# Decode attention over a cached K and V: the first load cut in two, a small load on another queue, the last loads in other pieces

## The chip, the cores and the metric

The kernel runs on one core of one Trainium2 chip. The metric is the device time of one execution in microseconds (us). The kernel before was run three times: 1307.24, 1308.48 and 1308.63 us, median 1308.48 us.

## The reference

One decode step for 2 sequences: attention with 32 heads of size 128 over a cache of 8192 positions, times a gate that an MLP computes, added to the input. All arrays are float32.

```python
def _A_ref(x, k_cache, v_cache, wq, wo):            # x: 2 x 1 x 512
    q = (x @ wq).reshape(B, Sq, 32, 128)             # heads first after a transpose
    scores = einsum("bhqd,bhkd->bhqk", q, k_cache) * (128 ** -0.5)
    p = softmax(scores, axis=-1)
    o = einsum("bhqk,bhkd->bhqd", p, v_cache)
    return o.reshape(B, Sq, 4096) @ wo
def _B_ref(x, w1, b1, w2, b2):                       # w1: 512 x 1376, w2: 1376 x 512
    h = gelu(layernorm(x) @ w1 + b1)
    return h @ w2 + b2
xn = layernorm(x)
out = x + _A_ref(xn, k_cache, v_cache, wq, wo) * silu(_B_ref(xn, w1, b1, w2, b2))
```

K and V hold 268 MB each, the weights another 22 MB. Each K and V element is used once, so a step is mostly the reading of them.

## The kernel before

**Tiles.** The 64 pairs of sequence and head are taken two at a time: 32 steps, each with one K tile and one V tile of 128 partitions x 128 positions x 128 floats (8.39 MB). Each half of the partitions holds one head, each partition 64 KB that lie in one piece in memory. A load moves one row per partition, and the 16 DMA engines share the 128 rows, 8 each.

**Buffers.** `kpool` has two buffers; wq, the 32 K tiles, one late V tile and wo take turns in them. `vpool` has one buffer. At the start it is `boot`, which holds w1, w2, x, b2 and scratch; then the V tiles follow in it. So k1 can be loaded when the projection of the queries (L241) has read wq, v0 when nothing uses `boot` any more, k2 when VectorE (DVE) is done with k0, v1 when TensorE (PE) is done with v0.

**A step** (L354 to L399). DVE multiplies K by the query in two halves (L279), sums over the head size (L284) and takes the maximum (L288). PE and ScalarE (ACT) turn that into exponentials (L305, L307, L312). PE multiplies them with V, 32 matmuls over 4 positions each (L327); `columns`, `spread` and `place` add the result into OA. The order of all instructions is written out by hand: each engine takes its own in the order of the program.

**Queues.** All large loads are issued by SyncE (SP) on its queue, in the order of the program: w1 (L98), the first 1280 rows of w2 (L99), the last 96 rows of w2 (L100), wq (L101), k0 in two halves, then k1, v0, k2, v1 and so on through `load` (L60). ACT issues five small ones on its own queue: x (L96), b1 and its tail (L107, L108), b2 (L109), and one row of the output at the end. A load waits on its issuing engine for whatever must be done before: the buffer's last reader, or a landing whose semaphore it uses again (there are eight of these for all loads).

**The start.** DVE and ACT compute two layer norms of x (L152 to L158; the square root L156 on ACT needs its function table loaded, as the copy L175 does before it). PE transposes the result, multiplies it with w1 (L196), DVE adds b1 and its tail (L202) and computes the gelu with a tanh from ACT (L207), PE multiplies with w2 (L215) and adds b2 (L218), ACT and DVE finish the gate. Then PE projects the queries from wq (L241), gathers them (L251) and spreads the first (L262); DVE's first multiply (L279) waits for that.

**The end.** The V tile of the last step is loaded in five pieces of 32, 32, 32, 16 and 16 positions (`PIECES`, L71), wo in five pieces of 8, 8, 8, 6 and 2 of its 32 rows per partition (`WO_PIECES`, L72; a row is 2 KB per partition, 262 KB in all). Each piece has its own semaphore, so the matmuls on it (L327, L419) start when it has landed. The final product (L419) takes 4 matmuls for each of the 32 rows of wo, 8 instructions in the trace; DVE multiplies by the gate and adds x (L423, L424), and SP and ACT write the two rows of the output (L427).

Of the kernel before, what the change touches and what calls it, by code (L numbers as in the profile page):

```python
# [8 lines left out]
F32 = mybir.dt.float32  # L9
AF = mybir.ActivationFunctionType  # L10
# [3 lines left out]
EPS = 1e-5  # L14
# [5 lines left out]
def decode_kernel(ctx: ExitStack, tc: tile.TileContext, x, kc, vc, wq, wo, w1, b1, w2, b2, out):  # L20
    nc = tc.nc
    P = 128
    B, H, S, DH = kc.shape
# [15 lines left out]
    NF = F // P  # L39
    FT = F - NF * P  # L40
# [4 lines left out]
    consts = ctx.enter_context(tc.tile_pool(name="consts", bufs=1))  # L45
    kpool = ctx.enter_context(tc.tile_pool(name="kpool", bufs=2))
    vpool = ctx.enter_context(tc.tile_pool(name="vpool", bufs=1))
    small = ctx.enter_context(tc.tile_pool(name="small", bufs=2))
# [9 lines left out]
    def load(dst, src, cuts):  # L58
        for a, e in zip(cuts, cuts[1:]):
            nc.sync.dma_start(dst[:, a:e], src[:, a:e])  # L60
# [5 lines left out]
    def load_v(n, cuts=(0, KP), pool=vpool, tag="v"):  # L66
        V[n] = pool.tile([P, KP, DH], F32, tag=tag, name=f"v{n}")
        load(V[n], vf[n], cuts)


    PIECES = (0, 32, 64, 96, 112, 128)  # L71
    WO_PIECES = (0, 8, 16, 24, 30, 32)  # L72


    wq_sb = kpool.tile([P, ND, H * DH], F32, tag="k", name="wq_sb")
# [3 lines left out]
    def take(p, n):  # L79
        a = used[0]  # L80
        used[0] += n
        assert used[0] <= KP * DH
        return boot[:p, a:a + n]

    w1_sb = take(P, ND * F).rearrange("p (c f) -> p c f", f=F)
    w2_sb = take(P, (NF + 1) * D).rearrange("p (c n) -> p c n", n=D)
    x_sb = take(B, D)
# [5 lines left out]
    z = take(P, P)  # L93
    th = take(P, P)

    nc.scalar.dma_start(x_sb, x.rearrange("b s d -> (b s) d"))  # L96

    nc.sync.dma_start(w1_sb, w1.rearrange("(p c) f -> p c f", p=P))  # L98
    nc.sync.dma_start(w2_sb[:, :NF, :], w2[:NF * P, :].rearrange("(p c) n -> p c n", p=P))  # L99
    nc.sync.dma_start(w2_sb[:FT, NF, :], w2[NF * P:, :])  # L100
    nc.sync.dma_start(wq_sb, wq.rearrange("(p c) n -> p c n", p=P))  # L101
    load_k(0, (0, KP // 2, KP))


    b1_sb = consts.tile([P, NF + 1], F32, name="b1_sb")
    nc.vector.memset(b1_sb, 0.0)
    nc.scalar.dma_start(b1_sb[:, :NF], b1[:NF * P].rearrange("(p c) -> p c", p=P))  # L107
    nc.scalar.dma_start(b1_sb[:FT, NF:NF + 1], b1[NF * P:, None])  # L108
    nc.scalar.dma_start(b2_sb, b2[None, :])  # L109
# [5 lines left out]
    nc.vector.memset(ones, 1.0)  # L115
    srow = consts.tile([1, HP], F32, name="srow")
    nc.vector.memset(srow, SCALE)
    eps_t = consts.tile([B, 1], F32, name="eps_t")
    nc.vector.memset(eps_t, EPS)

    mod = consts.tile([P, R], F32, name="mod")

# [231 lines left out]
    for n in range(N):  # L354
# [11 lines left out]
        if 1 <= n < LATE - 1 or n >= LATE:  # L366
# [7 lines left out]
            elif n == N - 1:  # L374
                load_v(N - 1, PIECES)
        if n >= LATE:
# [24 lines left out]
    wo_sb = kpool.tile([P, OC, D], F32, tag="k", name="wo_sb")  # L401
    load(wo_sb, wo.rearrange("(p c) n -> p c n", p=P), WO_PIECES)

# [51 lines left out]
```

## Time and profile before

| | before |
|---|---|
| median of 3 runs | 1308.48 us (1307.24 to 1308.63) |
| profiled execution, its own time | 1307.31 us |
| span in that execution, first to last instruction | 1305.5 us |
| DVE busy | 1128.8 us (86%) |
| PE busy | 444.4 us (34%) |
| ACT busy | 84.0 us (6%) |
| moved by DMA | 559.76 MB, mean 429 GB/s |
| PE's granted clock, mean | 0.629 of full speed |

The profile page is made from one execution. Its parts give the busy time of each engine, the span in 40 equal slices (each digit the busy tenths of a slice, then the DMA rate in GB/s), the DMA queues (q1 is SP's, q10 ACT's, q8 and q14 carry instructions), the chain of waits that ended last, the costliest groups of instructions, and the DMA issues with their size and the time from issue to landing. A row in order of time reads: start, duration, engine, line, operation, destination <- source, shape, count, and in brackets how long the engine was idle before and what ended that. SPq and ACTq rows are issues of DMAs, not transfers. A row of a stretch of time (such as 1.50:5.00) lists the busy time of PE, PE's weight loads, DVE, ACT and POOL, then PE's granted clock, the DMA engines' mean busy share and the rate in GB/s.

### The profile page before, as it was taken

Reading aid. Unit: us, or ns where it says so; the run is one execution under the profiler, and the core shown is the slowest. Engines: PE = TensorE matmul, PEld = TensorE weight load, DVE = VectorE, ACT = ScalarE, POOL = GpSimd, SP = SyncE. Lnnn points to the kernel's source line nnn. Section 1 sums busy time; section 2 is a strip of 40 time slices with the busy share of each in tenths; the row PEclk is TensorE's granted clock in tenths of the full one; section 3 lists DMA queues with packets and bytes.
Section 4 is the critical chain, followed back from the end, with each engine's and each line's share of the span. In section 5 each row is a group of like instructions: output and inputs, shape, how many; then the busy total and the mean of one; then the engine's idle time right before and its main releaser. Section 6 shows DMA issues by size and latency. Waiting matters only on the chain.

```text
span 1305.5 us, 7374 instructions
## 1 busy us (share of the span) xinstructions
PE 444.4 (34%) x3258; PEld 173.2 (13%) x3258; DVE 1128.8 (86%) x261; ACT 84.0 (6%) x276; POOL 2.8 (0%) x12
## 2 busy tenths in 40 slices
PE   6403333322333322333322333331333332231266
PEld 6101111111111101111100101110111101110013
DVE  1499989888889988889988888988888988889980
ACT  1100000000000000000000000000000000000000
POOL 0000000000000000000000000000000000000000
PEclk9756666556666656666655666655666655665668
DMA  9999999999999999999999999999999999999998
GB/s 398 440 424 442 424 442 422 442 424 442 424 442 424 438 430 436 432 434 432 432 436 428 440 426 438 428 440 424 440 426 440 424 444 422 446 404 426 438 416 339
DMA packets 11509, 559.76 MB, mean 429 GB/s; under 512 B 1515, under 2 KB 1523, under 8 KB 1750
## 3 DMA queue, kind: packets, MB, share of 16 engines
q1 hardware_dynamic: 11208, 559.29, 99.3%
q8 instruction: 25, 0.41, 0.1%
q10 hardware_dynamic: 270, 0.01, 0.0%
q14 instruction: 6, 0.05, 0.0%
HBM read 559.30 MB, written 0.00 MB: 428 GB/s over the span
## 4 chain that ended last, share of the span: by engine, by line
DMA 50%; DVE 48%; PE 1%; ACT 0%; issue 0%; SPq 0%; DVEq 0%
DMA k<-in_A_k_cache_dram 45%; DVE k L279 24%; DVE sc L284 24%; DMA wq_sb<-in_A_wq_dram 3%; DMA wo_sb<-in_A_wo_dram 2%; PE pq L241 1%; DVE nm L297 0%; ACT boot L244 0%; PE acc L419 0%; PE pqa L251 0%; SPq L60 0%; PE pb L262 0%; DVE mx L288 0%; SPq L100 0%; SPq L99 0%
## 5 line engine op out<-in xcount | busy, mean ns | idle before, releaser
L279 DVE TENSOR_TENSOR k<-k,q 128x8192 f32<-128x8192 f32 x64 | 555.5, 8681 | 109.7 <-DMA k<-in_A_k_cache_dram 98.0
L284 DVE TENSOR_REDUCE sc<-k 128x64 f32<-128x8192 f32 x64 | 552.4, 8666 | 0.0
L327 PE MATMUL po<-v,pz 128*8 128x512 f32 x2048 | 295.6, 742 | 202.3 <-DMA v<-in_A_v_cache_dram 202.3
L305 PE MATMUL pn<-nm,srow 1*64 1x1 f32 x128 | 11.7, 246 | 336.4 <-DVE nm L297 336.4
L327 PEld LDWEIGHTS po<-v,pz 128*8 128x8 f32 x2048 | 57.2, 104 | 422.8 <-DMA v<-in_A_v_cache_dram 213.7
L292 PE MATMUL pm<-ident,mx 128*1 128x128 f32 x32 | 11.8, 369 | 222.0 <-DVE Z L342 164.2
L305 PEld LDWEIGHTS pn<-nm,srow 1*64 1x64 f32 x128 | 9.0, 193 | 340.6 <-DVE nm L297 340.5
L334 ACT COPY o<-po 128x512 f32<-128x512 f32 x32 | 18.8, 586 | 516.3 <-PE po L327 516.3
L307 ACT COPY bias<-pn 128x1 f32<-128x1 f32 x32 | 5.1, 160 | 583.2 <-PE pn L305 583.2
L337 PE MATMUL pt<-mod,o 128*128 128x2 f32 x256 | 33.7, 254 | 22.9 <-ACT o L334 22.9
L337 PEld LDWEIGHTS pt<-mod,o 128*128 128x128 f32 x256 | 31.0, 191 | 52.6 <-ACT o L334 52.6
L318 PE MATMUL OA<-ones,ZR 128*128 128x1 f32 x64 | 18.6, 359 | 51.8 <-ACT ZR L315 51.8
L292 PEld LDWEIGHTS pm<-ident,mx 128*1 128x1 f32 x32 | 2.5, 79 | 224.4 <-issue 189.2
L312 ACT ACTIVATE pz<-sc,bias 64x128 f32<-64x128 f32 x64 | 25.5, 399 | 1.4
L318 PEld LDWEIGHTS OA<-ones,ZR 128*128 128x128 f32 x64 | 15.8, 307 | 54.5 <-ACT ZR L315 54.5
L262 PE MATMUL pb<-q_all,ident 64*64 64x128 f32 x128 | 21.6, 438 | 0.3 <-ACT q_all L253 0.3
L342 DVE TENSOR_TENSOR Z<-blk,pt 128x8 f32<-128x8 f32 x32 | 4.9, 152 | 18.4 <-PE pt L337 18.4
L196 PE MATMUL ph<-yT,boot 128*128 128x2 f32 (+1 forms) x88 | 19.5, 359 | 0.8 <-DMA boot<-in_B_w_dram 0.8
L196 PEld LDWEIGHTS ph<-yT,boot 128*128 128x128 f32 (+1 forms) x88 | 19.4, 317 | 0.9 <-ACT yT L166 0.9
L202 DVE TENSOR_TENSOR gh<-ph,b_sb 128x22 f32<-128x22 f32 x1 | 0.2, 181 | 21.0 <-PE ph L196 21.0
L350 PE MATMUL OA<-mod,Z 128*128 128x32 f32 x64 | 15.3, 332 | 4.4 <-DVE Z L342 4.3
L350 PEld LDWEIGHTS OA<-mod,Z 128*128 128x128 f32 x64 | 15.7, 304 | 4.8 <-DVE Z L342 4.8
(81 smaller groups left out, 119.5 us busy)
## 6 DMA issues: line engine op xcount, KB each, us to landing
k<-in_A_k_cache_dram SPq DMA_DIRECT2D x2, 4096.0 KB, 46.9
v<-in_A_v_cache_dram SPq DMA_DIRECT2D x3, 2048.0 KB, 19.2
wo_sb<-in_A_wo_dram SPq DMA_DIRECT2D x3, 2048.0 KB, 22.1
boot<-in_B_w_dram SPq DMA_DIRECT2D x1, 2752.0 KB, 9.7
boot<-in_B_w_dram SPq DMA_DIRECT2D x1, 2560.0 KB, 15.9
v<-in_A_v_cache_dram SPq DMA_DIRECT2D x2, 1024.0 KB
wo_sb<-in_A_wo_dram SPq DMA_DIRECT2D x1, 1536.0 KB
wo_sb<-in_A_wo_dram SPq DMA_DIRECT2D x1, 512.0 KB, 29.5
```

The costliest lines, as they stand in the source:

```text
L196: nc.tensor.matmul(ph[:w.shape[1], f * B:(f + 1) * B], w, yT[:, c, :], start=(c == 0), stop=(c == ND - 1))
L262: nc.tensor.matmul(p[HP * s:HP * (s + 1), :], w, q_all, start=True, stop=True)
L279: nc.vector.tensor_tensor(out=k, in0=k, in1=qb, op=ALU.mult)
L284: nc.vector.tensor_reduce(out=SC[n][:, a:e], in_=K[n][:, a:e, :], axis=AX.X, op=ALU.add)
L292: nc.tensor.transpose(p[:1, :], MX[n], ident)
L305: nc.tensor.matmul(p[HP * s:HP * (s + 1), :1], srow, nm[:, s:s + 1], start=True, stop=True)
L312: nc.scalar.activation(PZ[n % 3][r, :, s, :], sc[r], AF.Exp, bias=bias[r], scale=SCALE, accum_out=rs[r])
L318: nc.tensor.matmul(OA[:, b, OC:], ZR[:, a:a + P], ones[:, :1], start=False, stop=False)
L327: nc.tensor.matmul(po[R * j:R * j + U * JW, :], pz[:, t].rearrange("p s j -> p (s j)"), v[:, t * JW:(t + 1) * JW, :].rearrange("p j d -> p ...
L334: nc.scalar.copy(o4, PO[n % 2])
L337: nc.tensor.matmul(PT[n][:, :U], o4[:, i * DH:(i + 1) * DH], mod[:, i:U * JW:JW], start=(i == 0), stop=(i == JW - 1))
L350: nc.tensor.matmul(OA[:, b, :OC], Z[:, a:a + P], mod, start=False, stop=(n == N - 1))
```

## The change

Five edits, none to what is computed:

- w1 is loaded in two pieces: partitions 0 to 15 (one row for each of the 16 DMA engines), then 16 to 127.
- The last 96 rows of w2 go from SP's queue to ACT's, right behind x.
- `eps_t` is set first on DVE, and ACT computes a square root of it into a scratch tile ahead of everything else. With it the table for the square root is loaded ahead of x, whose load ACT issues next; the separate table load of the first copy (L175) is no longer in the program.
- V of the last step comes in two halves.
- wo comes in pieces of 16, 10, 4, 1 and 1 rows.

What the program makes of it: on ACT the order is table load, square root, x, w2's tail, b1, b1's tail, b2, then as before. On SP, wq now waits for the first piece of w1, the first half of k0 for x, the second for w2's tail, k1 for b1 (besides PE and what it waited for before); the last three wo pieces no longer wait for earlier landings. PE's and DVE's order is the same but for `eps_t`.

```diff
-    PIECES = (0, 32, 64, 96, 112, 128)
-    WO_PIECES = (0, 8, 16, 24, 30, 32)
+    PIECES = (0, 64, 128)
+    WO_PIECES = (0, 16, 26, 30, 31, 32)
...
-    nc.scalar.dma_start(x_sb, x.rearrange("b s d -> (b s) d"))
-
-    nc.sync.dma_start(w1_sb, w1.rearrange("(p c) f -> p c f", p=P))
+    w1_v = w1.rearrange("(p c) f -> p c f", p=P)
+    for p0, p1 in ((0, 16), (16, P)):
+        nc.sync.dma_start(w1_sb[p0:p1], w1_v[p0:p1])
     nc.sync.dma_start(w2_sb[:, :NF, :], w2[:NF * P, :].rearrange("(p c) n -> p c n", p=P))
-    nc.sync.dma_start(w2_sb[:FT, NF, :], w2[NF * P:, :])
     nc.sync.dma_start(wq_sb, wq.rearrange("(p c) n -> p c n", p=P))
     load_k(0, (0, KP // 2, KP))
...
+    eps_t = consts.tile([B, 1], F32, name="eps_t")
+    nc.vector.memset(eps_t, EPS)
     b1_sb = consts.tile([P, NF + 1], F32, name="b1_sb")
     nc.vector.memset(b1_sb, 0.0)
+    warm = small.tile([B, 1], F32, tag="warm", name="warm", bufs=1)
+    nc.scalar.activation(warm, eps_t, AF.Sqrt)
+    nc.scalar.dma_start(x_sb, x.rearrange("b s d -> (b s) d"))
+    nc.scalar.dma_start(w2_sb[:FT, NF, :], w2[NF * P:, :])
     nc.scalar.dma_start(b1_sb[:, :NF], b1[:NF * P].rearrange("(p c) -> p c", p=P))
     nc.scalar.dma_start(b1_sb[:FT, NF:NF + 1], b1[NF * P:, None])
     nc.scalar.dma_start(b2_sb, b2[None, :])
...
-    eps_t = consts.tile([B, 1], F32, name="eps_t")
-    nc.vector.memset(eps_t, EPS)
```

## The prediction

> **What bounds the kernel now.** I read the page from its second part on, then the chain, then both ends of the span in order of time. Lines (L202) are those of the kernel before.
>
> ```profile
> span 1305.5 us, 7374 instructions
> ...
> PE 444.4 (34%) x3258; PEld 173.2 (13%) x3258; DVE 1128.8 (86%) x261; ACT 84.0 (6%) x276; POOL 2.8 (0%) x12
> ...
> DMA  9999999999999999999999999999999999999998
> GB/s 398 440 424 442 424 442 422 442 424 442 424 442 424 438 430 436 432 434 432 432 436 428 440 426 438 428 440 424 440 426 440 424 444 422 446 404 426 438 416 339
> ...
> DMA 50%; DVE 48%; PE 1%; ACT 0%; issue 0%; SPq 0%; DVEq 0%
> ```
>
> The DMA row is full in every slice but the last, at 422 to 446 GB/s between the first and the last few: the kernel is one long stream of loads with a start and an end. The chain of waits names DVE for 48%, but only because it follows one load back through the instruction that freed its buffer. Two rows of the chain, two heads apart, give the pace:
>
> ```profile
> 154.73 8.69 DVE k L279
> ...
> 232.13 8.69 DVE k L279
> ```
>
> In 77.40 us two K and two V tiles pass, four loads of 8.39 MB: 19.35 us each, 433 GB/s, and 2.42 us for each of the 8 rows of 64 KB that one of 16 engines moves per tile. DVE needs about 35 of the 38.7 us that a head pair takes. So while a load always stands ready behind the running one, the time is start + stream + end, and a microsecond in which the engines move nothing, or move slowly, is a microsecond at the end. The span is 1305.5 us in an execution of 1307.31; the three runs have their median at 1308.48, 1.17 above it. I sum against 1307.31 and add 1.17.
>
> **The end: wo in other pieces.**
>
> ```profile
> 1276.58 9.45 PE L327 MATMUL po<-v,pz 128*8 128x512 f32 x64
> ...
> 1289.01 4.95 PE L419 MATMUL acc<-wo_sb,on 128*2 128x128 f32 x128 [0.52 <-DVE on L416]
> ...
> 1296.12 1.93 PE L419 MATMUL acc<-wo_sb,on 128*2 128x128 f32 x64 [2.16 <-DMA wo_sb<-in_A_wo_dram]
> ...
> 1299.80 1.93 PE L419 MATMUL acc<-wo_sb,on 128*2 128x128 f32 x64 [1.75 <-DMA wo_sb<-in_A_wo_dram]
> 1301.80 0.29 DVE L423 TENSOR_TENSOR res<-acc,gate 128x128 f32<-128x128 f32 x1 [12.84 <-PE acc L419]
> ```
> ```profile
> 1271.53 0.33 SPq L60 DMA_DIRECT2D wo_sb<-in_A_wo_dram  x1
> ```
> ```profile
> wo_sb<-in_A_wo_dram SPq DMA_DIRECT2D x1, 512.0 KB, 29.5
> ```
>
> PE does 8 wo rows in 1.93 us, 0.24 each. Before, rows 24 to 29 land at 1299.8 and the last two at 1271.53 + 29.5 = 1301.0, so PE ends 1301.73 and DVE starts at 1301.80. One wo row is 262 KB, 0.605 us of the stream. With 16, 10, 4, 1, 1: row 25 lands at 1299.8 - 4 x 0.605 = 1297.4, its ten rows are done at 1299.8; rows 26 to 29 land at 1299.8 and are done at 1300.8; row 30 lands at 1300.4, row 31 at 1301.0, done at 1301.27. **Gain 0.45 us.** The first 16 rows arrive in one piece, at 1299.8 - 14 x 0.605 = 1291.3 instead of half of them by 1289.0; 4.95 us of PE from there end at 1296.3, before row 25: nothing lost. V of the last pair in halves: PE starts it at 1276.58 and reaches its second half after some 5.5 us, at 1282; V is all there at 1301.0 - 32 x 0.605 = 1281.6. Even if that cover went, PE has 2.16 us of waiting for wo at 1296.12 to lose first. **0.** Three loads fewer are issued by SP, under a full queue: 0.
>
> **The start: a first load of 16 rows.** The first piece is 16 rows of 22 KB (0.35 MB), one for each engine, then 112 rows, where one load of 128 stood.
>
> ```profile
> 0.00:1.50 1.50, 0.00 (x0) 0.00 (x0) 0.49 (x8) 0.00 (x0) 0.90 (x8) 1.00 0.00 0
> 1.50:5.00 3.50, 1.23 (x10) 0.60 (x10) 1.93 (x6) 2.25 (x3) 1.94 (x6) 1.00 0.95 322
> 5.00:10.00 5.00, 1.27 (x8) 1.10 (x8) 2.70 (x9) 1.46 (x6) 0.00 (x0) 1.00 1.00 426
> ```
> ```profile
> 0.74 0.39 SPq L98 DMA_DIRECT2D boot<-in_B_w_dram  x1
> 0.74 0.54 ACTq L96 DMA_DIRECT2D boot<-in_A_x_dram  x1
> ```
> ```profile
> boot<-in_B_w_dram SPq DMA_DIRECT2D x1, 2752.0 KB, 9.7
> boot<-in_B_w_dram SPq DMA_DIRECT2D x1, 2560.0 KB, 15.9
> boot<-in_B_w_dram SPq DMA_DIRECT2D x1, 192.0 KB, 16.1
> ```
>
> In the first 5 us 3.5 x 322 = 1.13 MB move where the full rate would move 2.17: 2.4 us are missing. The issue stands at 0.74 and nothing moves for about a microsecond behind it, with either kernel; that leaves **0.7 us at most to gain**. The other end: no row of the trace shows 16 engines writing into 16 neighbouring partitions at once. In a full tile each engine fills 8 of the 128 partitions, at 27 GB/s (433/16), and the rows can't tell whether the engine or the way into those partitions sets that. If it is the way in, the 16 rows have two such shares to pass, 8 rows each of 0.81 us (22 KB at 27 GB/s): 6.5 us instead of 0.81, **5.7 lost**; and of the 112 rows after it fourteen shares get 8 and two get none, so they take 8 rows' time, not 7: 0.8 more. The nearest row is the one short transfer that there is, the 96-partition tail of w2: w2 lands at 1.19 + 15.9 = 17.1, wq at 2.12 + 35.78 = 37.9, and 8.59 MB in those 20.8 us are 1.0 us more than 433 GB/s needs. That leans to the way in, softly. I take the middle of the piece, 2.9, and the 0.8: **+3.7, bounds -0.7 and +6.5.**
>
> [...]
>
> **ACT's queue: table, x, w2's tail.**
>
> ```profile
> 2.72 1.28 ACT L175 ACT_TABLE_LOAD   x1 [2.72 <-DVE px L172]
> ...
> 4.29 1.28 ACT L156 ACT_TABLE_LOAD   x1
> 5.59 0.29 ACT L156 ACTIVATE sd_xn<-mv_xn,eps_t 2x1 f32<-2x1 f32 x1
> ...
> 10.53 19.49 PE L196 MATMUL ph<-yT,boot 128*128 128x2 f32 x88 [0.84 <-DMA boot<-in_B_w_dram]
> 30.06 0.18 DVE L202 TENSOR_TENSOR gh<-ph,b_sb 128x22 f32<-128x22 f32 x1 [20.97 <-PE ph L196]
> ...
> 36.16 0.40 PE L218 MATMUL pgate<-boot,ones 1*2 1x128 f32 x8
> ...
> 38.03 7.05 PE L241 MATMUL pq<-wq_sb,xnT 128*2 128x512 f32 x64 [1.48 <-DMA wq_sb<-in_A_wq_dram]
> ```
>
> One load of the table goes, and the other stands ahead of x: x is issued at about 0.74 + 1.28 + 0.29 = 2.3, four DMAs of ACT behind it. Layer norm starts later by that and more, as x meets busy engines, and gains 1.3 to 2 us at L156. L196 waited for w1 as well, so a microsecond or two reach PE; behind it stand L202, L215 and L241 on PE. What counts more is the order in the small queue. The trace shows how it is served:
>
> ```profile
> q1 hardware_dynamic: 62, 1.36, 97.4%
> q10 hardware_dynamic: 4, 0.00, 0.3%
> ```
> ```profile
> q1 hardware_dynamic: 76, 1.52, 95.3%
> q10 hardware_dynamic: 76, 0.00, 1.2%
> ```
>
> The first two rows are 1.5 to 5.5 us: 62 rows of SP's queue (q1), some 4 per engine, pass before ACT's (q10) gets b1 in. The others are 11.5 to 15.2 us: 76 and 76, one row of each in turn, whatever its size. Per engine ACT's queue now holds 6 rows of w2's tail, 8 of b1, 6 of b1's tail, and a count word behind each: 23 turns, the last behind turn 26 of SP's queue. That queue has 1 + 7 + 8 rows and 3 words before wq, so turn 26 is wq's seventh row of 2.42 us: **b1's tail lands near 35.5**, or 33 to 39 if it starts a turn sooner or later, and L202 needs it. From L202 to the end of L218 are 6.5 us, and PE, idle by then, runs its first 4 us at half clock:
>
> ```profile
> 50.00:52.00 2.00, 0.00 (x0) 0.00 (x0) 2.00 (x1) 0.20 (x1) 0.00 (x0) 0.50 1.03 442
> 96.00:100.00 4.00, 4.00 (x25) 0.88 (x28) 4.00 (x1) 0.27 (x1) 0.00 (x0) 0.50 1.14 492
> ```
>
> So L241 starts near 35.5 + 6.5 + 2 = 44 instead of 38.03: **6 us late** (4 to 9.5), and DVE's first multiply with it. Who waits: SP's loads that need a buffer freed.
>
> ```profile
> 2.79 42.67 SPq L60 DMA_DIRECT2D k<-in_A_k_cache_dram  x3
> ...
> 84.31 0.33 SPq L60 DMA_DIRECT2D k<-in_A_k_cache_dram  x1
> 105.59 0.33 SPq L60 DMA_DIRECT2D v<-in_A_v_cache_dram  x1
> ```
> ```profile
> k<-in_A_k_cache_dram SPq DMA_DIRECT2D x2, 4096.0 KB, 46.9
> ```
>
> The second half of k0, issued when w1 is in (0.74 + 9.7), lands at 57.3; k1, v0, k2 end at 76.7, 96.0, 115.4. With a microsecond from issue to data, k1 (issued by 45.46) has 10.8 us to spare, k2 10.7, and v1 8.8. Six us fit; 9.5 would open a gap of 0.7 at v1. **I take +0.3, bounds 0 and 3.** A late start of the stream moves both sides of this sum. On SP, wq now waits for the first piece, k0's halves for x and for w2's tail; those stand by 18 us at the latest, k0 is due at 37.9: 0.
>
> [...]
>
> **The sum:** -0.45 + 0 + 3.7 + 0.3 = +3.55; 1307.31 + 3.55 + 1.17 = **1312.0 us.**
>
> **The rivals.**
> 1. *The engines set the pace, not the partitions* (25%). For it: nothing but full tiles has been seen at rate. Then the piece only removes the ragged start, half of 0.7, the small queue stays covered, and wo gives 0.45: 1308.48 - 0.8 = **1307.7**, no slower. It decides at what 16 rows in 16 partitions cost: below 2.8 us the kernel is within 0.2%.
> 2. *The small queue outlasts the cover* (10%). b1's tail falls behind k0's rows and PE starts cold: L241 11.5 us late, v1's data 2.7 us after k2's end, k1's 0.7. With a free first piece 1308.48 - 0.8 + 2.7 = **1310.4**.
> 3. *Both* (8%): 1312.0 + 3 = **1315**.
> 4. *The change doesn't do what it says:* the table load saved and the early first row are off the path, since w1, wq and the stream come later; that is so in every case above and moves none.
>
> **How the numbers follow.** The forecast has 57%: from 1310 to 1315.8 by the term of the first piece. 0.2%, about what a measurement of this kernel can tell from no change, is 2.6 us: 1305.9 to 1311.1. Slower: four fifths of the forecast, all of rival 3, a third of rival 2, 0.57. Faster needs more than the 0.7 + 0.45 found here: 0.03. Within: 0.40. The range, 1307.5 to 1315.8, leaves out the lower half of rival 1 and the upper ends.
>
> **What would show it.** The first piece: the rate from 1.5 to 5 us falls well below 322 GB/s and w1 lands 3 us or more after 10.4; right for rival 1 if it lands at 10. The small queue: L202 waits for a DMA of b1 until 33 to 39, L241 starts 4 to 9.5 us after wq could let it. Cover: the DMA rate shows no hole near 57, 96 and 115. The end: the last L419 group after the last landing is 4 matmuls, not 64, and L423 starts 0.3 after it. A time under 1306 or over 1317 would make the whole reading wrong.

## The result, and the profile after

The changed kernel takes 1311.9 us (median of 7 runs, 1310.9 to 1312.68); the kernel before, on the same chip, takes 1307.81 us (7 runs, 1307.11 to 1308.95). The ratio is 1.0030, with a 95% interval of 1.0018 to 1.0042: 3.9 us slower (2.4 to 5.5). The profiled execution of the changed kernel took 1310.9 us, with a span of 1309.1.

In the page of the changed kernel, the line of DMA rates and the shares of the chain:

```profile
span 1309.1 us, 7373 instructions
...
GB/s 333 445 421 443 423 441 425 439 429 435 433 431 439 431 435 433 433 433 433 431 439 427 443 422 439 427 441 423 441 429 435 433 433 435 431 415 431 429 426 346
...
DVE 50%; DMA 46%; PE 3%; issue 1%; ACT 0%; SPq 0%; DVEq 0%
```

Only the first slice is clearly another one: 333 GB/s instead of 398. A slice is 32.7 us, so 65 GB/s are 2.1 MB, or 4.9 us of the stream. From the second slice on the stream runs as before. The table by stretches of the same kernel shows where in that slice it happened (last column GB/s, ahead of it the busy share of the DMA engines):

```profile
1.50:5.00 3.50, 0.69 (x2) 0.50 (x2) 1.10 (x4) 0.72 (x2) 1.94 (x6) 1.00 1.16 202
5.00:10.00 5.00, 1.24 (x12) 0.68 (x12) 3.21 (x10) 0.79 (x4) 0.00 (x0) 1.00 0.91 251
10.00:15.00 5.00, 0.64 (x4) 0.55 (x4) 0.34 (x2) 1.45 (x2) 0.00 (x0) 1.00 1.07 273
...
50.00:60.00 10.00, 8.20 (x80) 3.15 (x68) 0.09 (x1) 4.88 (x10) 0.00 (x0) 1.00 1.08 464
60.00:80.00 20.00, 0.15 (x4) 0.00 (x0) 19.72 (x3) 0.47 (x2) 0.00 (x0) 0.56 1.03 446
80.00:100.00 20.00, 0.37 (x1) 0.08 (x1) 19.97 (x4) 0.00 (x0) 0.00 (x0) 0.50 0.97 419
100.00:120.00 20.00, 11.14 (x82) 3.74 (x82) 20.00 (x4) 2.29 (x8) 0.00 (x0) 0.75 0.99 427
120.00:140.00 20.00, 1.01 (x7) 0.82 (x7) 19.97 (x7) 0.65 (x3) 0.00 (x0) 0.51 1.04 452
```

From 1.5 to 15 us the engines are as busy as before and move 202, 251 and 273 GB/s, where the kernel before moved 322, 426 and 430. The first two of these stand in the prediction; the third is:

```profile
10.00:15.00 5.00, 4.47 (x20) 4.50 (x21) 0.00 (x0) 1.20 (x1) 0.00 (x0) 1.00 1.01 430
```

(A row of a DMA counts whole in the stretch in which it starts, so a share can be over 1.) A busy engine that moves little is one whose rows take long: by the DMA records a row of w1 takes 1.99 us in the first sixteen and 1.15 to 1.98 in the groups of sixteen behind them, where the kernel before has 0.82 to 0.83 behind its first sixteen (1.52). So it is slow well past the first 16 rows: the 112 rows behind them are slow too. Around 57, 96 and 115 us there is no hole.

The start in order of time (start, duration, engine, line, operation, and in brackets the wait before it):

```profile
0.73 1.28 ACT L111 ACT_TABLE_LOAD   x1 [0.73 <-PEq L446]
0.89 0.55 ACTq L112 DMA_DIRECT2D boot<-in_A_x_dram  x1
...
5.91 0.68 DVE L157 BATCH_NORM_STATS2 st_xn<-boot 2x6 f32<-2x512 f32 x1 [3.26 <-DMA boot<-in_A_x_dram]
...
16.19 19.48 PE L201 MATMUL ph<-yT,boot 128*128 128x2 f32 x88 [5.24 <-DMA boot<-in_B_w_dram]
...
41.27 0.18 DVE L207 TENSOR_TENSOR gh<-ph,b_sb 128x22 f32<-128x22 f32 x1 [30.93 <-DMA b_sb<-in_B_b_dram]
...
43.08 4.87 PE L220 MATMUL pgate<-boot,hT 128*2 128x128 f32 x88 [7.40 <-issue]
...
48.41 7.18 PE L246 MATMUL pq<-wq_sb,xnT 128*2 128x512 f32 x64
```

The lines are those of the kernel before plus 5. The matmuls on w1 (L201) start at 16.19 instead of 10.53, and they wait for w1. DVE's addition of b1 (L207) waits for b1 until 41.27, and L246 begins at 48.41 instead of 38.03 without a wait of its own: it stands behind PE's other work. About 5 us of these 10 are the stream's own delay: with the split alone the same line starts at 43.00 (next section). Where DVE is bound by the stream again, the delay is 4.23 us (232.13 before):

```profile
236.36 8.69 DVE L284 TENSOR_TENSOR k<-k,q 128x8192 f32<-128x8192 f32 x1 [1.41 <-DMA k<-in_A_k_cache_dram]
```

The end of the changed kernel, in order of time:

```profile
1295.28 4.99 PE L424 MATMUL acc<-wo_sb,on 128*2 128x128 f32 x128 [3.69 <-DMA wo_sb<-in_A_wo_dram]
1301.30 2.07 PEld L424 LDWEIGHTS acc<-wo_sb,on 128*2 128x2 f32 x80 [1.33 <-DMA wo_sb<-in_A_wo_dram]
...
1303.78 0.98 PEld L424 LDWEIGHTS acc<-wo_sb,on 128*2 128x2 f32 x40 [0.41 <-DMA wo_sb<-in_A_wo_dram]
1305.07 0.11 PEld L424 LDWEIGHTS acc<-wo_sb,on 128*2 128x2 f32 x8 [0.31 <-DMA wo_sb<-in_A_wo_dram]
1305.54 0.29 DVE L428 TENSOR_TENSOR res<-acc,gate 128x128 f32<-128x128 f32 x1 [13.49 <-PE acc L424]
```

The last wait for wo ends at 1305.07 and the addition of the gate follows at 1305.54, against 1301.80 before: 3.74 us later, half a microsecond less than the stream's 4.23.

### The profile page after: what moved, and what is told of

Its sections match the earlier page's. It is cut to its first block, busy times and chain, and to the rows that moved or that the text cites. A ratio compares the mean times of both kernels' runs of the same rounds, so it can differ in the third digit from the quotient of the medians.

```text
span 1309.1 us, 7373 instructions
## 1 busy us (share of the span) xinstructions
PE 445.4 (34%) x3258; PEld 173.1 (13%) x3258; DVE 1128.7 (86%) x261; ACT 82.7 (6%) x276; POOL 2.8 (0%) x12
## 4 chain that ended last, share of the span: by engine, by line
DVE 50%; DMA 46%; PE 3%; issue 1%; ACT 0%; SPq 0%; DVEq 0%
DMA k<-in_A_k_cache_dram 42%; DVE k L284 25%; DVE sc L289 25%; DMA wo_sb<-in_A_wo_dram 2%; PE ph L201 1%; DMA boot<-in_B_w_dram 1%; PE pq L246 1%; PE pgate L220 0%; DVE nm L302 0%; ACT boot L249 0%; PE acc L424 0%; PE pqa L256 0%; PE pgate L223 0%; DVE Z L347 0%; DVE mx L293 0%
## 5 line engine op out<-in xcount | busy, mean ns | idle before, releaser
L207 DVE TENSOR_TENSOR gh<-ph,b_sb 128x22 f32<-128x22 f32 x1 | 0.2, 181 | 30.9 <-DMA b_sb<-in_B_b_dram 30.9
L201 PE MATMUL ph<-yT,boot 128*128 128x2 f32 (+1 forms) x88 | 19.5, 359 | 5.2 <-DMA boot<-in_B_w_dram 5.2
L201 PEld LDWEIGHTS ph<-yT,boot 128*128 128x128 f32 (+1 forms) x88 | 19.4, 317 | 5.3 <-issue 5.3
```

Source lines behind the costliest of these rows:

```text
L201: nc.tensor.matmul(ph[:w.shape[1], f * B:(f + 1) * B], w, yT[:, c, :], start=(c == 0), stop=(c == ND - 1))
```

## The experiments

Two theories stood against each other. **A:** the way into the partitions. A load of few or unluckily chosen partitions takes longer than the engines need, and the whole stream moves back by that. **B:** ACT's queue. w2's tail ahead of b1 makes the gate late, and the late start costs. Each kernel was timed beside the kernel before on the same chip, whose medians were 1307.4 to 1307.7 us.

### The split alone, and everything but the split

On the kernel before:

```diff
-    nc.sync.dma_start(w1_sb, w1.rearrange("(p c) f -> p c f", p=P))
+    w1_v = w1.rearrange("(p c) f -> p c f", p=P)
+    for p0, p1 in ((0, 16), (16, P)):
+        nc.sync.dma_start(w1_sb[p0:p1], w1_v[p0:p1])
```

> The kernel before with one edit: w1 in two loads, 16 rows and 112 rows. Theory A (the way into the partitions: few neighbouring partitions take less than the sixteen engines can give) has nearly the whole difference here: w1 lands 5 to 6 us after 10.4, every later load 4 to 5 us later than before without a hole, time 1307.8 + 4.5 = 1312.3 (1311.3 to 1313.3). Theory B (the loss comes from ACT's queue: w2's tail and b1 behind it, the late L241) has nothing here: w1 by 10.4 to 10.9, time 1307.8 within 0.7.

Measured: 1312.33 us against 1307.53; ratio 1.0034 (1.0022 to 1.0047), 4.4 us. The two rows of the timeline that answer to 10.53 and 38.03 before:

```profile
15.52 19.49 PE L198 MATMUL ph<-yT,boot 128*128 128x2 f32 x88 [5.81 <-DMA boot<-in_B_w_dram]
...
43.00 8.62 PE L243 MATMUL pq<-wq_sb,xnT 128*2 128x512 f32 x64 [0.74 <-DMA wq_sb<-in_A_wq_dram]
```

w1 is 5 us late, and so is wq: 43.00 - 38.03 = 4.97 us. The stream hardly gets any of it back: the multiply that starts at 232.13 in the kernel before starts at 236.66 here, 4.53 us later.

The reverse, the changed kernel with w1 in one load:

```diff
-    w1_v = w1.rearrange("(p c) f -> p c f", p=P)
-    for p0, p1 in ((0, 16), (16, P)):
-        nc.sync.dma_start(w1_sb[p0:p1], w1_v[p0:p1])
+    nc.sync.dma_start(w1_sb, w1.rearrange("(p c) f -> p c f", p=P))
```

> The changed kernel with w1 in one load again, all else kept. Theory A: w1 lands at 10 to 11, b1's tail near 36 and L246 some 5 to 6 us later than in the kernel before, no hole near 57, 96 and 115, and the end gains its 0.4 to 0.9: 1307.2 (1306.4 to 1308). Theory B: 1311 to 1312, as the changed kernel, with holes at k1 or v1.

Measured: 1307.87 us; ratio 1.0000 (0.9991 to 1.0008). The gate is late here as well, by b1's tail and by nothing else:

```profile
38.18 0.18 DVE L205 TENSOR_TENSOR gh<-ph,b_sb 128x22 f32<-128x22 f32 x1 [28.95 <-DMA b_sb<-in_B_b_dram]
...
45.12 7.05 PE L244 MATMUL pq<-wq_sb,xnT 128*2 128x512 f32 x64
```

L244 starts 7.1 us later than in the kernel before, and the time is the same. Theory B falls as the reason for the 3.9 us: the split alone holds the loss. But the expected 0.6 us of gain are not to be seen either, so a smaller cost of ACT's edits could be hidden by the gain of the end; that is asked further down.

### Which partitions, not how many loads

w1 in two loads of 64 partitions, `((0, 64), (64, P))` in place of `((0, 16), (16, P))`:

> The kernel before with w1 in two loads of 64 partitions each. Both loads are wide enough to feed all sixteen engines with four rows each. Theory A, carried over by its own price (a row of 22 KB takes 0.81 us when its share of the partitions is its own, and half of the shares stand idle in each load): up to twice the 6.5 us that w1 needs, w1 lands 4 to 6.5 us after 10.4 and the time is 1307.8 + 4 to 6.5 = 1312 to 1314.3. Rival C (what costs is a load with one row per engine, or 112 rows that don't divide into 8 per engine, not the partitions): w1 within 0.7 of 10.4, time 1307.8 within 0.7.

Measured: 1314.63 us; ratio 1.0052 (1.0040 to 1.0065), 6.8 us. Its rates by stretch:

```profile
1.50:5.00 3.50, 1.23 (x10) 0.60 (x10) 1.93 (x6) 2.25 (x3) 1.95 (x6) 1.00 0.93 215
5.00:10.00 5.00, 1.27 (x8) 1.10 (x8) 2.70 (x9) 1.46 (x6) 0.00 (x0) 1.00 0.99 207
10.00:15.00 5.00, 0.00 (x0) 0.00 (x0) 0.00 (x0) 1.20 (x1) 0.00 (x0) 1.00 1.01 207
```

207 GB/s, half of the 426 of the kernel before, with all sixteen engines busy.

Two loads again, but cut by columns, each of all 128 partitions:

```diff
-    nc.sync.dma_start(w1_sb, w1.rearrange("(p c) f -> p c f", p=P))
+    w1_v = w1.rearrange("(p c) f -> p c f", p=P)
+    for c0, c1 in ((0, ND // 2), (ND // 2, ND)):
+        nc.sync.dma_start(w1_sb[:, c0:c1], w1_v[:, c0:c1])
```

> The kernel before with w1 in two loads as well, but each of all 128 partitions and half of the columns (11 KB per row). Theory A: all partitions are reached in both loads, so nothing is lost: w1 at 10.4 within 0.7, time 1307.8 within 0.7. Rival D (a second load in front costs by itself, through its issue or its completion): some of the 4.5 us shows here too, 1309 or more.

Measured: 1307.87 us; ratio 1.0001 (0.9992 to 1.0009). A second load in front costs nothing that can be told from zero (-1.0 to 1.2 us).

Two loads of 64 rows again, even partitions first, then odd ones. If it counts which partitions a load reaches, they can move at another rate than the halves; if only the dealing of 64 rows to the engines counts, it is 207 GB/s again:

```diff
-    nc.sync.dma_start(w1_sb, w1.rearrange("(p c) f -> p c f", p=P))
+    w1_v = w1.rearrange("(p c) f -> p c f", p=P)
+    for p0 in range(2):
+        nc.sync.dma_start(w1_sb[p0:P:2], w1_v[p0:P:2])
```

> The kernel before with w1 in two loads of 64 rows, as in the halves that gave 207 GB/s, but the even partitions first and the odd ones second. [...]

Measured: 1310.38 us; ratio 1.0022 (1.0013 to 1.0030), 2.9 us, less than half of the 6.8 us of the halves. The timeline has two facts:

```profile
10.28 0.36 SPq L101 DMA_DIRECT2D boot<-in_B_w_dram  x1
...
10.33 19.48 PE L198 MATMUL ph<-yT,boot 128*128 128x2 f32 x88 [0.64 <-DMA boot<-in_B_w_dram]
...
40.63 9.17 PE L243 MATMUL pq<-wq_sb,xnT 128*2 128x512 f32 x64 [4.60 <-DMA wq_sb<-in_A_wq_dram]
```

w1 is there at 10.3, as in the kernel before: the alternating partitions cost nothing. What costs is a wait that the edit brought along: SP issues w2 (L101) only at 10.28, when w1 has landed (1.19 before, and 1.98 with the two halves). So the program as built lets w2 wait for the strided pieces; the likely reason, not shown, is that they share its buffer. The queue runs dry, wq is 2.6 us late, and that is about the time.

Eight loads of 16 rows, eight partitions apart, `w1_sb[p0:P:8]` for `p0` in 0 to 7:

> The kernel before with w1 in eight loads of 16 rows, one for each engine as in the first piece of the change, but eight partitions apart (0, 8, 16 and so on; then 1, 9, 17). If a way into the partitions serves 8 neighbours, each of the 16 rows has its own: 426 GB/s, w1 at 10.4 within 1, 1307.8 within 0.7 (or a little more for eight issues). [...] If one row per engine in a load costs by itself: slower than the halves.

Measured: 1316.98 us; ratio 1.0073 (1.0060 to 1.0085), 9.5 us, against 6.8 us for the halves.

```profile
5.00:10.00 5.00, 1.27 (x8) 1.10 (x8) 2.70 (x9) 1.46 (x6) 0.00 (x0) 1.00 1.08 229
...
15.00:20.00 5.00, 3.19 (x15) 3.22 (x15) 0.00 (x0) 0.00 (x0) 0.95 (x1) 1.00 0.58 176
```
```profile
16.81 19.49 PE L198 MATMUL ph<-yT,boot 128*128 128x2 f32 x88 [7.11 <-DMA boot<-in_B_w_dram]
...
47.16 8.49 PE L243 MATMUL pq<-wq_sb,xnT 128*2 128x512 f32 x64 [3.68 <-DMA wq_sb<-in_A_wq_dram]
```

The first of these is about half the rate again (229 GB/s against 426); the second has the idle queue (0.58) of a wait like the one just told: SP issues w2 at 16.50. w1 is 6.3 us late, wq 9.1, so the wait adds some 2.9. So 16 rows eight apart do not have a way each. Nor does one row per engine cost by itself: w1 is no later than with the halves (6.8 us late there), and the rest is the wait. The three runs have 207 GB/s with 64 neighbours, w1 in time with every second partition (10.33 us), and 229 GB/s with every eighth; which partitions share a way they do not show.

The DMA records of w1's rows, sixteen at a time in order of their start, say the same by durations (mean us of a row of 22 KB; the first sixteen include the start of the queue):

| kernel | rows 1-16 | 17-32 | the other six groups |
|---|---|---|---|
| before | 1.52 | 0.83 | 0.82 |
| even, then odd partitions | 1.35 | 0.83 | 0.82 |
| eight apart | 1.28 | 1.61 | 1.49 to 1.69 |
| halves of 64 | 1.31 | 1.71 | 1.58 to 1.73 |
| 16 rows, then 112 | 2.01 | 1.93 | 1.06 to 1.41 |

Two of these kernels begin with 16 rows, one for each engine. Eight partitions apart these rows take 1.28 us, as 16 neighbours 2.01 us: with the same number of rows and engines, it is the partitions that count.

### The price of the 16 rows and of the 112 rows

The last line of the table has two parts, and the prediction priced them separately. On the kernel before, the first 16 rows of w1 are loaded once more ahead of w1, into k0's buffer, where k0 overwrites them later:

```diff
+    K[0] = kpool.tile([P, KP, DH], F32, tag="k", name="k0")
+    w1_16 = w1.rearrange("(p c) f -> p (c f)", p=P)[:16].rearrange("p (j d) -> p j d", d=DH)
+    nc.sync.dma_start(K[0][:16, :ND * F // DH], w1_16)
     nc.sync.dma_start(w1_sb, w1.rearrange("(p c) f -> p c f", p=P))
...
-    load_k(0, (0, KP // 2, KP))
+    load(K[0], kf[0], (0, KP // 2, KP))
```

> The kernel before, with the first 16 rows of w1 loaded once more ahead of w1, into k0's buffer, where nothing reads them and k0 overwrites them; w1 itself stays one load of 128. This prices the 16-row piece alone, without the 112 rows. [...] If one way serves 8 neighbours: 6.5 us, 1314.2. If the engines set the pace: 0.8 us, 1308.5.

Measured: 1309.72 us; ratio 1.0017 (1.0008 to 1.0025), 2.2 us.

```profile
40.23 7.05 PE L244 MATMUL pq<-wq_sb,xnT 128*2 128x512 f32 x64 [1.47 <-DMA wq_sb<-in_A_wq_dram]
```

wq is 2.20 us late, between the 0.8 of the engines' pace and the 6.5 of one way for 8 neighbours. The bytes need 0.8 us: 1.4 us of price. The DMA records show where it went: rows 1 to 16 take 2.02 us each and rows 17 to 32, the first of w1 behind the piece, 1.92, where the kernel before has 1.52 and 0.83; from there on it is 0.82 again. So the rows behind the piece lose time too. And the first sixteen rows take 1.52 us in the kernel before as well, so part of the piece's time may fall into the start of the queue; that is likely, but not shown.

The same with `[16:]`, rows 16 to 127:

> The kernel before, with rows 16 to 127 of w1 loaded once more ahead of w1, into k0's buffer, where nothing reads them; w1 itself stays one load of 128. At the full rate 112 rows of 22 KB (2.47 MB) take 5.7 us. The run with the 16 rows alone shifted the stream by 2.2 us, 1.4 more than 16 rows at the full rate, and the split by 5.0: so the 112 rows should cost 3.5 us above their full rate. If they do so by themselves (112 rows from partition 16 on are dealt in such an order that several engines meet in one way): the stream shifts by 9.2 us, 1307.4 + 9.2 = 1316.6 (1315.9 to 1317.3). If only behind a 16-row piece, whose engines go on out of step: 5.7 to 6.5 us, 1313.1 to 1313.9. The prediction's 0.8 above the full rate would also be 1313.9.

Measured: 1317.0 us; ratio 1.0070 (1.0056 to 1.0084), 9.2 us. The start of the projection, and below it a line of the page's DMA issues (KB, then us from issue to landing):

```profile
47.05 7.05 PE L244 MATMUL pq<-wq_sb,xnT 128*2 128x512 f32 x64 [0.98 <-DMA wq_sb<-in_A_wq_dram]
```
```profile
k<-in_B_w_dram SPq DMA_DIRECT2D x1, 2408.0 KB, 12.5
```

wq is 9.02 us late, for 5.7 us of bytes: 3.3 us of price. The 112 rows land 12.5 us after their issue, where all 128 took 9.7: seven eighths of the bytes take longer than the whole. They do it by themselves, with no 16-row piece ahead of them. Their records have 1.2 to 1.4 us for a row. Together 1.4 + 3.3 = 4.7, close to the 4.97 of the split.

Why 112 rows are slow is not shown. The author's estimate is that engines meet by chance on the way into the partitions; rows between the 0.82 us of the load of 128 and the 1.7 of the loads of 64 fit that. No record names the partition that it wrote, and no run tells the number 112 from the start at partition 16.

### The end, and ACT's queue

The two lists of pieces alone, on the kernel before:

```diff
-    PIECES = (0, 32, 64, 96, 112, 128)
-    WO_PIECES = (0, 8, 16, 24, 30, 32)
+    PIECES = (0, 64, 128)
+    WO_PIECES = (0, 16, 26, 30, 31, 32)
```

> The kernel before with the edits of the end alone: V of the last pair in halves, wo in 16, 10, 4, 1, 1 rows. The term of the prediction: 4 matmuls instead of 16 behind the last landing, 0.45 us less: 1307.8 - 0.45 = 1307.3 (1306.9 to 1307.8), in the profile the addition of the gate 0.3 us after the last group's landing and not 0.7 to 0.8; the start as before (w1 10.4, wq 37.9). Rival: V in halves or 16 rows of wo at once delay what stands behind them, and the end comes no earlier: 1307.8 or more, with a wait for V ahead of the last pair's matmuls.

Measured: 1306.1 us against 1307.72; ratio 0.9989 (0.9980 to 0.9998), 1.4 us faster (0.3 to 2.6). It is the fastest kernel of the study, though by less than 0.2%. Three rows of its timeline: the same stream-bound multiply as above, the last weight load for wo and the addition of the gate:

```profile
231.65 8.69 DVE L279 TENSOR_TENSOR k<-k,q 128x8192 f32<-128x8192 f32 x1 [3.66 <-DMA k<-in_A_k_cache_dram]
...
1300.04 0.11 PEld L419 LDWEIGHTS acc<-wo_sb,on 128*2 128x2 f32 x8 [0.29 <-DMA wo_sb<-in_A_wo_dram]
...
1300.51 0.29 DVE L423 TENSOR_TENSOR res<-acc,gate 128x128 f32<-128x128 f32 x1 [13.15 <-PE acc L419]
```

The gate's addition is 1.29 earlier than 1301.80, of which 0.48 is scatter of the stream (231.65 against 232.13). That leaves 0.8, and the addition starts 0.47 behind the last wait for wo, where it was 2.0 before. Three other executions have the new pieces; set against the same multiply, their addition is 0.5 us earlier (the changed kernel), 0.4 earlier (without the split) and 0.1 later (with the table load, below). So a profile tells the gain only to some half a microsecond.

The edits at ACT alone (table load, x, w2's tail), with w1 and the end as in the kernel before:

> The kernel before with the edits at ACT alone: the table load ahead of x, and w2's tail over ACT's queue ahead of b1. The prediction's term: b1's tail near 36, L246 6 us late, covered, 0 to 0.3. Against the run without the split, which stood 1.8 us above the run with the end's edits alone: if these edits cost that, 1307.7 + 1.0 to 1.8 = 1308.7 to 1309.5, with the loads from k0 on 0.6 to 0.8 us later than in the kernel before; if that was scatter, 1307.7 within 0.5.

Measured: 1308.77 us; ratio 1.0006 (0.9997 to 1.0015), 0.8 us (-0.4 to 2.0): unclear. In its profiled execution, at 1310.65 the longest of its runs, the stream is 0.17 late (the multiply at 232.30 instead of 232.13), but the addition of the gate comes at 1305.13, 3.33 late. That is made at the very end (the last row is the kernel before):

```profile
1297.81 2.62 PE L422 MATMUL acc<-wo_sb,on 128*2 128x128 f32 x64 [2.97 <-DMA wo_sb<-in_A_wo_dram]
1301.47 3.60 PE L422 MATMUL acc<-wo_sb,on 128*2 128x128 f32 x64 [1.05 <-DMA wo_sb<-in_A_wo_dram]
```
```profile
1300.00:1302.00 2.00, 0.95 (x20) 0.40 (x16) 0.00 (x0) 0.00 (x0) 0.00 (x0) 0.50 0.12 49
1302.00:1306.00 4.00, 3.07 (x60) 1.81 (x49) 0.58 (x2) 0.00 (x0) 0.00 (x0) 0.54 0.00 1
```
```profile
1300.00:1302.00 2.00, 1.73 (x64) 1.35 (x54) 0.20 (x1) 0.00 (x0) 0.00 (x0) 1.00 0.02 6
```

One half of it is that PE can begin with the last pieces only at 1301.47, 1.67 later than in the kernel before; why they come so late the profile doesn't show. The other half is PE: 64 matmuls take 3.60 us at a granted clock of 0.50 to 0.54 (the column ahead of the DMA share); the kernel before had 1.93 in its execution, at 1.00. So the old pieces leave enough work behind the last landings that PE's clock decides over some 1.7 us. With the new ones only 4 matmuls stand there.

The edits of the end with the table load, and w2's tail on SP's queue:

> The edits of the end and the table load ahead of x, but w2's tail on SP's queue as before and w1 in one load. If w2's tail on ACT's queue is what cost: b1 in by 16, the addition of b1 behind the matmuls of w1 near 30, and 1307.7 - 1.0 to 1.6 = 1306.1 to 1306.7, as with the end's edits alone. If the table load or the later x costs: 1307.5 or more.

Measured: 1306.86 us; ratio 0.9992 (0.9983 to 1.0001). It lies between the run with the end's edits alone and the run without the split, and its interval touches both. Whether w2's tail on ACT's queue costs anything is not settled by these times.

### How far the late gate is covered

On the kernel before, b1's tail goes over SP's queue between the halves of k0:

```diff
-    load_k(0, (0, KP // 2, KP))
...
+    K[0] = kpool.tile([P, KP, DH], F32, tag="k", name="k0")
+    load(K[0], kf[0], (0, KP // 2))
+    nc.sync.dma_start(b1_sb[:FT, NF:NF + 1], b1[NF * P:, None])
+    load(K[0], kf[0], (KP // 2, KP))
...
-    nc.scalar.dma_start(b1_sb[:FT, NF:NF + 1], b1[NF * P:, None])
```

> The kernel before with the 96 last values of b1 loaded over SP's queue between the two halves of k0, so that they land near 47.7 whatever else is done: a stronger dose of the late L241 of the changed kernel. By the margins of the prediction (k1 10.8, k2 10.7, v1 8.8 us) L241 starts at 47.7 + 6.5 to 7.2 = 54.2 to 54.9, 16.2 to 16.9 us late; the stream gets a hole of 5 to 6 us at k1 and 2 to 3 more at v1, 7.4 to 8.1 in sum: 1307.8 + 7.8 = 1315.6 (1314 to 1317). Rival: the late start is caught up elsewhere or the margins are larger than read, no hole and 1307.8; or they are smaller, and the whole 16 us show: 1324.

Measured: 1317.97 us; ratio 1.0082 (1.0069 to 1.0096), 10.7 us (9.0 to 12.6), about a microsecond above the expected range. The timeline, then the rates by stretch (the last row is the kernel before):

```profile
54.41 7.05 PE L243 MATMUL pq<-wq_sb,xnT 128*2 128x512 f32 x64
...
61.51 0.33 SPq L60 DMA_DIRECT2D k<-in_A_k_cache_dram  x1
```
```profile
55.00:57.00 2.00, 2.00 (x27) 0.44 (x19) 0.83 (x4) 0.15 (x1) 0.00 (x0) 1.00 0.08 25
57.00:62.00 5.00, 5.00 (x50) 1.54 (x43) 0.00 (x0) 2.79 (x5) 0.00 (x0) 1.00 0.00 0
...
95.00:115.00 20.00, 3.98 (x23) 1.59 (x27) 19.97 (x5) 1.71 (x7) 0.00 (x0) 0.50 0.91 383
```
```profile
95.00:115.00 20.00, 11.13 (x78) 3.51 (x78) 20.00 (x3) 1.21 (x4) 0.00 (x0) 0.76 0.98 424
```

The projection starts at 54.41, 16.4 us late, as expected, and the hole stands where the margins put it: at k1, then again (383 GB/s instead of 424) ahead of v1. It is some 2 us deeper than expected at k1: by the DMA records 15 of the 16 engines had finished their rows of k0 by 55.5 (a busy share of 0.08 from 55 to 57), some 2 us ahead of the landing at 57.3 from which the prediction counted the margin. So cover is real and ends; the changed kernel, with 5 to 6 us of lateness against its stream, stays inside it.

## Why the prediction was right, step by step

The forecast was 1312.0 and 1311.9 was measured, slower as said. The cause was right: the two loads that w1 was cut into move slower than the engines could (202 to 273 GB/s from 1.5 to 15 us, 322 to 430 before), and the whole stream moves back by that. That the figures agree to 0.1 us is luck, three times over. The two sizes in the start's term were wrong and cancelled; the 2.9 in it was the middle between nothing and 5.7, which no row gave; and the change was forecast at +3.55 from 1308.48, while 3.9 (2.4 to 5.5) was measured from 1307.81.

- **The start's term, +3.7, was 4.4 to 5.0, with its parts the wrong way round.** The 16 rows were priced at 2.9 and cost 1.4; the 112 rows were priced at 0.8 and cost 3.3. The prediction gave the 112 rows one row's time more and assumed that the engines would otherwise keep out of each other's way, as in a load of 128, where a row takes 0.82 us. In a load of 112 a row takes 1.2 to 1.4; that the engines meet is the author's estimate of the reason, not shown. The one row that hinted at it, w2's tail of 96 partitions, was used for the 16 rows only and not for the 112.
- **The ways were taken for groups of 8 neighbours.** The run with every eighth partition rules that out: each of its 16 rows would have had a way of its own, and the rate was 229 GB/s, about half. No run shows the two ways that the prediction gave the 16 rows, nor the 6.5 us at the most that followed from them: loaded ahead of w1, these rows moved wq back by 2.20 us.
- **The end's -0.45 lies within what was measured:** -0.8 to +0.1 in four profiled executions, -1.4 (-2.6 to -0.3) in the times of the end's edits alone, where the forecast is near the upper end. The groups behind the landings came as worked out, the addition 0.47 behind the last wait instead of 0.3. What was missed is that the 1.93 us for 8 rows were taken at a granted clock of 1.00: in one execution here it was 3.60, at 0.50 to 0.54. V in halves made PE wait 0.67 us inside the last step; it then waited 3.69 us for wo, so that cost nothing, as said.
- **ACT's queue, +0.3, can't be told from zero (0.8, -0.4 to 2.0).** b1's tail came at 38.2 without the split, at the late end of 33 to 39 (at 41.3 in the changed kernel, where the delay of the split comes on top; the prediction's sign did not count that in). So the trace agrees with one row of each queue in turn, as the records from 11.5 to 15.2 us in the kernel before have it (76 of each). Without the split L241 was 7.1 us late, not 6: b1's tail came 2.7 us behind the 35.5, and from there to L241 it took 6.9 us instead of 8.5, as PE did not run L215 at half clock after its idle time (7.40 us in the changed kernel; the clock was 1.00 from 35 to 50 us). Nor was x issued at 2.3, but at 0.89, while the table load still ran. Why b1's tail came later all the same is not shown.
- **The cover** held, without a hole, as said. By the run with the late b1 its margin at k1 is some 2 us smaller than the prediction's 10.8.
- **Profile to median, +1.17**, was 1.0 in the changed kernel (1310.9 and 1311.9).
- **The rivals.** That the engines set the pace fell at the 207 GB/s with all engines busy, against 426 with the same engines and all partitions. The small queue did not outlast its cover.

The parts, each alone, are 4.4 (split), -1.4 (end) and 0.8 (ACT): 3.8, and the whole change is 3.9. Each carries 1.2 to 1.6 us either way: the split is clear of zero, the end barely, ACT not.

## What to carry to other kernels

Cut a load along the free dimension and not into blocks of partitions: two loads of all 128 partitions cost nothing here (ratio 1.0001), two of 64 neighbours halved the rate (207 GB/s against 426), and 112 rows took longer than 128 (12.5 us from issue to landing against 9.7). In a kernel that is one stream of loads, what is lost at its head is found again at its end: of the 4.97 us by which the split alone made wq late, 4.4 were in the time. So price a new first load by the rate at which it will move, not by its bytes. Late work beside the stream is free up to a margin: the projection of the queries 7.1 us late cost nothing that the time shows (ratio 1.0000, with the end's edits in it), 16.4 us late it cost 10.7. That margin ends when the queue runs dry, here some 2 us ahead of the landing of the last load.

## What the runs showed of the hardware

- A row of 22 KB takes an engine 0.82 us in a load of 128 partitions, 1.7 in a load of 64 neighbours, and 1.2 to 1.4 in a load of 112, while the engine counts as busy all the time: the busy share (1.00 with 128 partitions, 0.99 with 64, 0.95 with 112, from 5 to 10 us) hardly shows this, only the GB/s beside it (426, 207, 242).
- ACT's sequencer issued x at 0.89 us, inside a table load that ran from 0.73 to 2.01.
- After 7.4 us without a matmul PE still had a granted clock of 1.00 at 43 us; in the last wo pieces of another execution it had 0.50 to 0.54.
